# The next pair's first two mask products moved to one place, one of them in a score bank

## The chip, the cores and the metric

The kernel runs on one core of a Trainium2 chip. The metric is the time of one execution on the device, in microseconds (us). Four runs of the kernel before took 996.92 to 997.95 us, with a median of 997.31 us.

## What is computed

The reference has two stages. The first is routed attention over 4 batches, 8 heads, 768 positions and 64 dimensions. Each query and each key is assigned to the nearest of 16 centroids of its head, and a query sees only the keys of its own cluster. The second stage is a wide layer with the gate h * erf(softplus(h)).

```python
q_assign = np.argmax(np.einsum('bhsd,hcd->bhsc', q_n, c_n), axis=-1)
k_assign = np.argmax(np.einsum('bhsd,hcd->bhsc', k_n, c_n), axis=-1)
mask = q_assign[:, :, :, None] == k_assign[:, :, None, :]
scores = np.where(mask, scale * np.matmul(q, k.transpose(0, 1, 3, 2)), -1000000000.0)
attn = np.exp(scores - np.max(scores, axis=-1, keepdims=True))
attn = attn / (np.sum(attn, axis=-1, keepdims=True) + 1e-09)
x = np.matmul(attn, v)                      # then (3072, 512)
h = x @ w_in                                # (3072, 2048)
out = (h * erf(np.maximum(h, 0) + np.log1p(np.exp(-np.abs(h))))) @ w_out
```

## The kernel before

**Pairs, units, periods.** Two heads are worked on at a time, one on rows 0 to 63 and one on rows 64 to 127: 16 pairs, numbered p = 0 to 15. A pair has 12 units, one for each half of the 768 queries (384) and each block of 128 keys. `period` (line 756) does two units, u and u + 1, so a pair has six periods, i = 0 to 5; the text calls them the first to the sixth. The attention takes the first 400 us or so of the span; the wide layer follows and is not touched by the change.

**The order of the work is written out by hand.** Every instruction of the attention goes through `InOrder` (line 54, its call on line 62), which keeps program order on each engine. So almost every row of the profile says L62, and rows are told apart by their tiles. There is no scheduler that moves them.

**The mask as a product.** Cluster membership enters the scores as a second, small matrix product that is added to the first. For a query, `qm` holds its one-hot cluster code. For a key, `km` holds a very large negative number at all clusters but its own. `masks` (line 357) makes a half (384 columns) of `qm` or `km` of the next pair. A product of the constant `pick` with `hotT`, the one-hot codes turned on their side, puts the codes into a bank of the accumulation memory (PSUM), and the function returned then copies them from there into `qm` or `km`, in bf16. For queries the product reads rows 0 to 63 of the array, for keys rows 64 to 127. With `narrow` it reads only 32 of these rows, which lie beside those that other small products use.

**Banks.** PSUM has eight banks here: `turned[0]` and `turned[1]`, one each; `ps_s`, two buffers `sc` of two banks each for the score units; and `wide`, two banks. `turned[0]` and `turned[1]` in turn hold the attention sums of the two halves, the transposed maxima and the mask products.

**One period**, in program order:

- `turn` in the first and fourth periods: the row maxima found for the next half are transposed on TensorE and copied into one row of `qm` for each head, on ScalarE ("CAST qm<-turned 1x384").
- `step_ahead(u)`: for a block of queries of the half to come, bf16 products `wide<-kv,qv` and `wide<-km,qm`, and then a maximum over them on VectorE ("TENSOR_REDUCE nmx<-wide").
- `products` (line 431) of u and of u + 1: the fp32 products of queries and keys ("sc<-qT,kT"), for each head on its own 64 rows. An fp32 product runs in two passes and loads its own weights.
- `step_ahead(u + 1)` in three pieces, with the mask part `scores` (line 444) of u and of u + 1 between them ("sc<-qm,km").
- `curve` (line 458): the exponential on ScalarE ("ACTIVATE pr<-sc"), one for each unit.
- `accumulate` on GpSimd and `attend` on TensorE ("turned<-pr,in_v") for the two units of the period before.

The four mask products of the next pair are put in by the table `MASKS` (line 50): the first key half in the first period (place 3, between the scores of u and u + 1, in `turned[0]`, narrow, and copied by VectorE), the first query half in the third (place 0, ahead of the products, in `turned[1]`, copied by ScalarE), the second key half in the third and the second query half in the sixth (place 2, narrow, copied by ScalarE). The first pair has its own table, `FIRST_MASKS`.

**Weight steps.** Beside the attention, 22 pieces of the wide layer's weights are fetched and brought into another number form, two pieces in a pair, up to pair 11: `size` and `rest` on ScalarE, `bounded` and `shifted` on VectorE, `sign` on ScalarE, `summed` on GpSimd, which then has the next piece fetched. For piece n1 = 2p - 1, `size` and `rest` stand at the end of the second period, `bounded`, `sign` and `shifted` in the fourth and `summed` in the fifth.

Of the kernel before, what the change touches and what calls it, by code (L numbers as in the profile page):

```python
# [9 lines left out]
F32 = mybir.dt.float32  # L10
# [4 lines left out]
ALU = mybir.AluOpType  # L15
# [4 lines left out]
P = 128  # L20
# [10 lines left out]
NPAIR = B * HP  # L31
# [12 lines left out]
BIG = 2.0**60  # L44
# [2 lines left out]
NPT = NJ + 2  # L47
N_LATE = 10
LAST_X = 11
MASKS = {(0, 3): ("k", 0), (2, 0): ("q", 0), (2, 2): ("k", 1), (5, 2): ("q", 1)}  # L50
FIRST_MASKS = {(2, 0): ("k", 0), (2, 1): ("q", 0), (2, 2): ("k", 1), (5, 2): ("q", 1)}


# [17 lines left out]
def kernel(  # L71
# [13 lines left out]
    te, ve, ae, ge = (  # L85
        InOrder(tc, e, in_order) for e in (nc.tensor, nc.vector, nc.scalar, nc.gpsimd)
    )
# [8 lines left out]
    turned = [ps.tile([P, 512], F32, name=f"turned{i}") for i in range(2)]  # L96
# [12 lines left out]
    def passing(name, bufs, **kw):  # L109
        return attention.enter_context(tc.tile_pool(name=name, bufs=bufs, **kw))  # L110

    ps_s = passing("ps_s", 2, space=PSUM)
# [12 lines left out]
    nbig = const.tile([P, 1], F32, name="nbig")  # L125
# [71 lines left out]
    for base, pattern, sign, op, fill in (  # L197
# [5 lines left out]
            out=first, in_=first, compare_op=op, fill=fill, base=base, pattern=pattern,  # L203
# [31 lines left out]
    def size(n):  # L235
        ae.activation(out=w_steps[n][0], in_=steps[n][0], func=ACT.Abs, scale=UP)

    def rest(n):
        lo = steps[n][1]
        ae.activation(out=lo.bitcast(I32), in_=lo.bitcast(U32), func=ACT.Copy, scale=2.0**-29)  # L240

    def size_and_rest(n):
        size(n)
        rest(n)
# [109 lines left out]
        if p < NPAIR:  # L354
            ae.copy(out=pairs[p][nm + "v"], in_=pairs[p][nm + "T"])

    def masks(p, nm, half, bank, narrow=False, copied_by=ae):

        if p >= NPAIR:
            return lambda: None  # L360
        st = pairs[p]
        cols = slice(half * HW, (half + 1) * HW)
        r = slice(0, D) if nm == "q" else slice(D, P)
        if narrow:
            r = slice(r.start + half * Q, r.start + (half + 1) * Q)
        won = bank[:, 0:HW]
        te.matmul(won, lhsT=pick[r, half], rhs=st["hotT"][r], start=True, stop=True)
        if nm == "q":
            return lambda: ae.activation(out=st["qm"][:, cols], in_=won, func=ACT.Relu)
        if copied_by is ve:  # L370
            return lambda: ve.tensor_scalar(
                out=st["km"][:, cols], in0=won, scalar1=BIG, scalar2=nbig, op0=ALU.mult, op1=ALU.add
            )
        return lambda: ae.activation(
            out=st["km"][:, cols], in_=won, func=ACT.Identity, bias=nbig, scale=BIG
        )
# [3 lines left out]
    def maxima_step(p, i, sm=wide, behind=False):  # L380

        st = pairs[p]
        nmx = maxima[p % 2]
        t, half = divmod(i, 2)

        def passes(a, b, start, rows):
            for e in range(2):
                r = slice(e * D + rows.start, e * D + rows.stop)
                te.matmul(
                    sm[:, e, 0:HW], lhsT=st[a][r, t * P : (t + 1) * P],  # L390
                    rhs=st[b][r, half * HW : (half + 1) * HW], start=start, stop=not start,
                )

        passes("qv", "kv", True, slice(0, D))
        if behind:
            yield
        passes("qm", "km", False, slice(Q, D) if behind else slice(0, D))
        if behind:
            yield
        ve.tensor_reduce(  # L400
            out=nmx[:, :, t, half], in_=sm[:, :, 0:HW], axis=AX.X, op=ALU.max, negate=True
        )
        if i in (NJ - 1, 2 * NJ - 1):
            h = i // NJ
            ve.tensor_reduce(
                out=lowest[h][:, :, ::D].rearrange("p t e -> p e t"),
                in_=nmx[:, :, h * HJ : (h + 1) * HJ], axis=AX.X, op=ALU.min,
            )
            turns.append((p, h))
# [17 lines left out]
    units = [(p, half, j) for p in range(NPAIR) for half in range(2) for j in range(NJ)]  # L427

    sc_of = {}

    def products(u):
        p, half, j = units[u]
        if u in sc_of:
            return
        st = pairs[p]
        sc = sc_of[u] = ps_s.tile([P, 2, 512], F32, name="sc", tag="s")
        for e in range(2):
            r = slice(e * D, (e + 1) * D)
            te.matmul(
                sc[:, e, 0:HW], lhsT=st["kT"][r, j * P : (j + 1) * P],  # L440
                rhs=st["qT"][r, half * HW : (half + 1) * HW], start=True, stop=False,
            )
# [300 lines left out]
    def step_ahead(u, behind=False):  # L743
        p, i = divmod(u + NJ, 2 * NJ)
        steps = maxima_step(p, i, behind=behind) if p < NPAIR else iter(())
        if not behind:
            run(steps)
        return steps
# [7 lines left out]
    def period(p, i):  # L756
        u = 2 * NJ * p + 2 * i
        n1, n2 = 2 * p - 1, 2 * p
        early = lambda n: 0 <= n < N_EARLY

        def mask(place):
            which = (MASKS if p else FIRST_MASKS).get((i, place))
            if which:
                return masks(p + 1, *which, turned[0 if i in (0, 5) else 1], place > 1, ve if place == 3 else ae)
            return lambda: None

        if u > 0:
            for which in turns if i in (0, 3) else ():
                turn(*which)
                turns.remove(which)  # L770
            step_ahead(u)
        mask(0)()
        next(part[0], None)
        if i == 0 and p:
            run(routing[0])
        if u == 2:
            next(routing[0])
        products(u)
        products(u + 1)
        mask(1)()  # L780
        second = step_ahead(u + 1, True) if u > 0 else iter(())
        next(second, None)
        scores(u)
        next(second, None)
        mask(3)()
        next(second, None)
        next(part[0], None)
        scores(u + 1)
        later = mask(2)
        if i == 3:  # L790
            similarities(p + 2)
            routing[0] = choose(p + 2, sc_of[u + 1][:, 0])
        curve(u)
        later()
        curve(u + 1)
        if u == 0:
            step_ahead(1)
            similarities(1)
            routing[0] = choose(1, turned[0])
            next(routing[0])  # L800
            next(routing[0])
            vectors(1, "q")
            vectors(1, "k")
        if i == 0 and early(n1 - 1):
            bounded(n1 - 1)
            shifted(n1 - 1)
            sign(n1 - 1)
        elif i == 1 and early(n1):
            size_and_rest(n1)
        elif i == 3 and early(n1):  # L810
            bounded(n1)
            sign(n1)
        elif i == 5 and early(n2):
            rest(n2)
        for _ in range(min(len(forms), FORMS.get(p, {}).get(i, 0))):
            forms.pop(0)[0]()
        if i == 3:
            next(routing[0], None)
            if early(n1):
                shifted(n1)  # L820
            for _ in range(2):
                next(routing[0], None)
        elif i == 1:
            load(p + 1, "v", v, vp)
            if p == 0:
                run(routing[0])
                transposes(2, "q")
        elif i == 2:
            transposes(p + 2, "k")
        elif i == 4:  # L830
            vectors(p + 2, "k")
            vectors(p + 2, "q")
        elif i == 5:
            transposes(p + 3, "q")
        if u > 0:
            if i == 1 and early(n1 - 1):
                summed(n1 - 1)
            elif i == 4 and early(n1):
                summed(n1)
            for w in (u - 2, u - 1):  # L840
                accumulate(w)
            if i % HJ == 1 and p in POOL_FORMS and forms:
                forms.pop(0)[1]()
            for w in (u - 2, u - 1):
                attend(w)
            if i % HJ == 0:
                part[0] = divide(u - 1)
                next(part[0])
        if i == 3 and early(n2):
            size(n2)  # L850
# [11 lines left out]
    st = pairs[0]  # L862
    st["qT"], st["kT"] = rows[0]["q"], rows[0]["k"]
    ve.transpose(out=st["qT"], in_=st.pop("q").rearrange("p n t -> p (n t)"))
    for e in range(2):
        ve.tensor_copy(
            out=ccT[e * D : (e + 1) * D, :, e * C : (e + 1) * C],
# [8 lines left out]
    for r in (0, D):  # L876
        for half in range(2):
            for e in range(2):
                c = r + half * Q + e * C
                ve.tensor_copy(  # L880
                    out=pick[r : r + D, half, e * D : (e + 1) * D].rearrange("p (n c) -> p n c", n=2)[:, :, 1 : C + 1],
# [5 lines left out]
    run(choose(0))  # L887
    copies = [
        masks(0, nm, half, bank)
        for nm, half, bank in (("q", 0, wide[:, 0]), ("k", 0, turned[0]), ("k", 1, turned[1]))  # L890
    ]
# [30 lines left out]
    u = len(units)  # L922
# [107 lines left out]
```

## Time and profile before

| | us |
|---|---|
| median of four runs | 997.31 |
| the profiled execution | 997.32 |
| its span in the trace | 995.6 |
| TensorE matmuls busy (PE) | 987.6 (99%) |
| TensorE weight loads busy (PEld) | 743.0 (75%) |
| VectorE busy (DVE) | 700.8 (70%) |
| ScalarE busy (ACT) | 488.1 (49%) |
| GpSimd busy (POOL) | 350.3 (35%) |

The profile is that of one execution. Times are counted from the start of its span. A row of the timeline gives the start, the time from there to the end of the last instruction merged into it, the engine, the line, the operation, the tile written and the tiles read, shapes and count; in brackets stands how long the engine had been idle, and what ended that. A matmul's time reaches to the end of its way through the array, so back-to-back matmuls overlap in it, and products on different rows of the array run beside each other. Pairs 1 to 11 show the same rows, shifted by 24.59 us from pair to pair; the rows quoted later are mostly those of pairs 3 and 4.

### The profile page before, as it was taken

To read this page: it belongs to the slowest core of one execution; us is meant where nothing else is said; L and a number is where in the kernel's file an instruction comes from. 1 tells how busy PE (TensorE), PEld (TensorE's weight loads), DVE (VectorE), ACT (ScalarE), POOL (GpSimd) and SP (SyncE) were. 2 spreads that over 40 slices of the span, in tenths; PEclk is the share of its full clock that TensorE was granted. 3 is DMA by queue.
4 is the path that set the end of the run, shared out by engine and by line. 5 is a ranking of instruction groups with operands and counts; after the bars stand their busy time and mean duration, and the time that the engine had idled before them with its cause. 6 is when DMAs were issued, how large, how long until landed. Compare 5 with 4: busy or idle time off the path is not lost.

```text
span 995.6 us, 20543 instructions
## 1 busy us (share of the span) xinstructions
PE 987.6 (99%) x8362; PEld 743.0 (75%) x8362; DVE 700.8 (70%) x1347; ACT 488.1 (49%) x659; POOL 350.3 (35%) x237
## 2 busy tenths in 40 slices
PE   8999999999999999999999999999999999999998
PEld 3555555555555555688888888888888888888887
DVE  8888888888888776779676554756475647655653
ACT  3777777777776665475532324150505050505050
POOL 1677878778878888662400000000000000000000
PEclk9999999999999999999999999999999999999999
DMA  9444444444444210232000100010001000000001
GB/s 222 78 111 108 108 108 110 112 112 104 96 96 110 51 36 18 99 109 65 1 12 32 42 1 22 22 43 1 22 22 43 1 21 22 1 1 22 22 1 42
DMA packets 147294, 55.88 MB, mean 56 GB/s; under 512 B 128640, under 2 KB 137088, under 8 KB 147200
## 3 DMA queue, kind: packets, MB, share of 16 engines
q1 hardware_dynamic: 144848, 54.29, 21.8%
q8 instruction: 65, 1.06, 0.5%
q10 hardware_dynamic: 2352, 0.30, 0.2%
q14 instruction: 29, 0.24, 0.1%
HBM read 41.98 MB, written 12.58 MB: 55 GB/s over the span
## 4 chain that ended last, share of the span: by engine, by line
PE 96%; DVE 1%; POOL 1%; DMA 1%; issue 0%; ACT 0%; SPq 0%; ACTq 0%; DVEq 0%; POOLq 0%
PE bank L62 43%; PE turned L62 31%; PE sc L62 16%; PE wide L62 6%; POOL more_out L62 1%; DVE nmx L62 1%; DMA g_more<-in_moe_w_out_dram 0%; DMA in_q<-in_q_dram 0%; DVE sims L62 0%; POOL x_more L62 0%; DVE kT L62 0%; DVE qT L62 0%; ACT pr L62 0%; ACT w_out L62 0%; DVE turned L62 0%
## 5 line engine op out<-in xcount | busy, mean ns | idle before, releaser
L62 POOL TENSOR_TENSOR more_out<-more_out,pr 128x768 f32<-128x768 f32 x128 | 217.0, 1695 | 19.2 <-ACT pr L62 10.5
L62 DVE TENSOR_REDUCE nmx<-wide 128x2 f32<-128x768 f32 x189 | 180.7, 956 | 58.7 <-PE wide L62 57.6
L62 ACT ACTIVATE pr<-sc 128x768 f32<-128x768 f32 x192 | 148.9, 812 | 95.7 <-PE wide L62 91.0
L62 PE MATMUL turned<-pr,in_v 128*32 128x194 f32 x3072 | 145.5, 330 | 0.0
L62 PEld LDWEIGHTS turned<-pr,in_v 128*32 128x32 f32 x3072 | 91.5, 109 | 51.2 <-issue 21.3
L62 DVE TENSOR_TENSOR g<-bank,g 128x256 f32<-128x256 f32 x222 | 89.7, 422 | 53.2 <-PE bank L62 46.4
L62 PE MATMUL bank<-x_own,w_in 128*128 128x256 f32 x424 | 104.7, 380 | 1.1 <-DVE g L62 1.1
L62 PE MATMUL bank<-w_out,g 128*128 128x256 f32 x448 | 103.1, 379 | 0.0
L62 PE MATMUL sc<-qT,kT 64*128 64x384 f32 x528 | 98.3, 484 | 0.0
L62 PEld LDWEIGHTS bank<-w_out,g 128*128 128x128 f32 x448 | 85.1, 190 | 11.6
L62 PEld LDWEIGHTS bank<-x_own,w_in 128*128 128x128 f32 x424 | 80.3, 190 | 12.9 <-DVE g L62 1.5
L62 DVE TENSOR_TENSOR osb<-bank,osb 128x256 f32<-128x256 f32 x87 | 35.5, 421 | 72.8 <-ACT osb L62 25.4
L62 ACT COPY g<-bank 128x256 f32<-128x256 f32 x28 | 10.4, 372 | 153.0 <-PE bank L62 148.5
L62 ACT ACT_TABLE_LOAD x48 | 61.6, 1283 | 45.7 <-DVE g L62 45.1
L62 PE MATMUL bank<-x_more,more_in 128*128 128x256 f32 x296 | 76.0, 379 | 0.0
L62 POOL TENSOR_TENSOR more_out<-pr,pr 128x768 f32<-128x768 f32 x32 | 60.0, 1875 | 28.4 <-ACT pr L62 28.4
L62 PEld LDWEIGHTS sc<-qT,kT 64*128 64x128 f32 x528 | 51.8, 187 | 19.8 <-ACT inv L62 2.3
L62 PE MATMUL wide<-kv,qv 64*128 64x384 bf16 x378 | 64.9, 328 | 1.1 <-ACT km L62 0.6
L62 PEld LDWEIGHTS <-qv 64*128 64x128 bf16 x384 | 26.9, 93 | 51.8 <-issue 35.7
L62 PE MATMUL bank<-more_out,g_more 128*128 128x256 f32 x272 | 64.3, 379 | 0.0
L62 DVE TENSOR_TENSOR g<-a_s,g 128x512 f32<-128x512 f32 x96 | 62.5, 689 | 1.4 <-ACT a_s L62 1.4
L62 PE MATMUL wide<-km,qm 64*128 64x384 bf16 (+1 forms) x378 | 62.5, 327 | 0.0
(170 smaller groups left out, 1668.3 us busy)
## 6 DMA issues: line engine op xcount, KB each, us to landing
x_own<-in_moe_w_in_dram SPq DMA_DIRECT2D x13, 512.0 KB, 4.2
in_v<-in_v_dram SPq DMA_DIRECT2D x32, 192.0 KB, 3.0
x_dram<-more_out SPq DMA_DIRECT2D x128, 48.0 KB, 1.7
x_own<-x_dram SPq DMA_DIRECT2D x6, 1024.0 KB, 5.3
out_dram<-osb SPq DMA_DIRECT2D x23, 256.0 KB, 2.0
in_k<-in_k_dram SPq DMA_DIRECT2D x59, 96.0 KB, 2.7
in_q<-in_q_dram SPq DMA_DIRECT2D x58, 96.0 KB, 2.8
g_more<-in_moe_w_out_dram SPq DMA_DIRECT2D x6, 512.0 KB, 3.4
```

The lines of the kernel that those rows point to most:

```text
L62: ins = getattr(self.engine, name)(*args, **kw)
```

## The change

The first key mask leaves the first period and is put beside the first query mask, in the third period, ahead of the products. The query mask's product no longer goes to `turned[1]` but to the first bank of the score buffer of u, which is allocated early for it; the key mask's goes to `turned[1]`, on all 64 of its rows. Both are copied by ScalarE, the query's first. As u's fp32 product overwrites the bank of the query mask, the period's two products are made in turned order, that of u + 1 first. This holds for pairs 1 to 14; the first pair's table is unchanged, and the last pair makes no masks.

Two weight steps on ScalarE move with it, in the pairs that have them: `size` from the end of the second period to behind the two copies in the third, and `rest` to the fourth, ahead of its products. The copy by VectorE goes away, and so does the piece of `step_ahead` that made room for it: the order of the remaining instructions is the same there.

```diff
-MASKS = {(0, 3): ("k", 0), (2, 0): ("q", 0), (2, 2): ("k", 1), (5, 2): ("q", 1)}
+MASKS = {(2, 2): ("k", 1), (5, 2): ("q", 1)}
...
-        if copied_by is ve:
-            return lambda: ve.tensor_scalar(
-                out=st["km"][:, cols], in0=won, scalar1=BIG, scalar2=nbig, op0=ALU.mult, op1=ALU.add
-            )
...
         passes("qm", "km", False, slice(Q, D) if behind else slice(0, D))
-        if behind:
-            yield
...
+    multiplied = set()
+
+    def bank_of(u):
+        if u not in sc_of:
+            sc_of[u] = ps_s.tile([P, 2, 512], F32, name="sc", tag="s")
+        return sc_of[u]
...
     def products(u):
         p, half, j = units[u]
-        if u in sc_of:
+        if u in multiplied:
             return
+        multiplied.add(u)
         st = pairs[p]
-        sc = sc_of[u] = ps_s.tile([P, 2, 512], F32, name="sc", tag="s")
+        sc = bank_of(u)
...
-        products(u)
-        products(u + 1)
+        both = i == 2 and 0 < p < NPAIR - 1
+        if both:
+            copies = [masks(p + 1, "q", 0, bank_of(u)[:, 0]), masks(p + 1, "k", 0, turned[1])]
+            for copy in copies:
+                copy()
+            if early(n1):
+                size(n1)
+        if i == 3 and early(n1):
+            rest(n1)
+        for w in (u + 1, u) if both else (u, u + 1):
+            products(w)
         mask(1)()
         second = step_ahead(u + 1, True) if u > 0 else iter(())
         next(second, None)
         scores(u)
-        next(second, None)
-        mask(3)()
         next(second, None)
...
-        elif i == 1 and early(n1):
-            size_and_rest(n1)
```

More of the change, by code (lines that the diff above doesn't have):

```diff
@@ L355, in vectors, with masks @@
             ae.copy(out=pairs[p][nm + "v"], in_=pairs[p][nm + "T"])
-    def masks(p, nm, half, bank, narrow=False, copied_by=ae):
+    def masks(p, nm, half, bank, narrow=False):
         if p >= NPAIR:
@@ L763, in mask @@
             if which:
-                return masks(p + 1, *which, turned[0 if i in (0, 5) else 1], place > 1, ve if place == 3 else ae)
+                return masks(p + 1, *which, turned[0 if i in (0, 5) else 1], place > 1)
             return lambda: None
```

## The prediction

> **What bounds the kernel now.** I read the page's chain of work that ended last first, then the busy table of chosen stretches, then the timeline of single periods.
>
> ```profile
> span 995.6 us, 20543 instructions
> PE 96%; DVE 1%; POOL 1%; DMA 1%; issue 0%; ACT 0%; SPq 0%; ACTq 0%; DVEq 0%; POOLq 0%
> ```
>
> TensorE is 96% of the chain that ended last, and its granted clock is at the top digit in all 40 slices. So a change counts by what it adds to or takes from TensorE's own stream. Copies on ScalarE and VectorE count only where TensorE waits for them.
>
> The edit acts in 14 pairs (p = 1 to 14), in the first and the third of their six periods. What the two mask products cost there is seen by setting pair 4 beside pair 15, which has no next pair and so no masks. The stretches run from one period's first score product (qm with km) to the next period's; columns: stretch, its length, then busy time of each engine.
>
> ```profile
> 118.81:123.06 4.25, 4.25 (x63) 2.44 (x61) 3.69 (x8) 3.28 (x5) 1.91 (x2) 1.00 0.61 114
> 388.49:392.58 4.09, 4.09 (x63) 2.34 (x63) 2.90 (x5) 2.30 (x4) 2.92 (x3) 1.00 0.00 0
> 123.06:126.99 3.93, 3.93 (x55) 2.50 (x54) 2.96 (x5) 3.01 (x5) 3.80 (x3) 1.00 0.87 225
> 392.58:396.34 3.76, 3.76 (x54) 2.08 (x53) 2.92 (x5) 1.51 (x2) 3.31 (x3) 1.00 0.11 27
> ```
>
> The first two rows hold the key mask of the first period: 4.25 against 4.09, so it costs 0.16 us. The last two hold the query mask of the third period: 3.93 against 3.76, about 0.16 us too. TensorE is busy throughout all four, though pair 15 gives VectorE 0.8 us less to do in the first of them: nothing else waits there.
>
> **Removed: the key mask's place in the first period.** It goes from between the scores to beside the query mask: 14 x 0.16 = 2.24 us off the path. Its copy on VectorE (14 x 0.62 us) was off the path: the maxima that stood behind it ended at 120.91, and TensorE came to the next product into that bank at 121.19. Taking it away is worth nothing.
>
> **Added beside the query mask: the key mask, on the other 64 rows.** The set-up at the start shows such a pair.
>
> ```profile
> 11.29 0.32 PE L62 MATMUL wide<-hotT,pick 64*128 64x384 bf16 x1
> 11.30 0.50 PE L62 MATMUL turned<-hotT,pick 64*128 64x384 bf16 x2
> ```
>
> Three mask products: the query one on rows 0 to 63 and a key one on rows 64 to 127 start within 0.01 us, and only the third comes 0.17 later. So the second mask is taken at nothing beyond the 0.16 that the query mask pays today. In today's third period the upper rows just run 0.16 us ahead for that time and wait at the period's end.
>
> **Added: a wait.** The query mask now lies in the first half of unit u's score bank, so u's product may overwrite it only after ScalarE has copied it. The turned order puts u+1's product in front as cover. How long is the copy, and how long the cover? In pairs 12 to 14 ScalarE has no weight steps, and the same copy starts as soon as the mask is there, as it will after the change:
>
> ```profile
> 322.00 0.32 PE L62 MATMUL turned<-hotT,pick 64*128 64x384 bf16 x1
> 322.36 0.49 ACT L62 ACTIVATE qm<-turned 128x384 bf16<-128x384 f32 x1 [0.62 <-PE turned L62]
> ```
>
> With M for the mask's start, the copy runs from M + 0.36 to M + 0.85. TensorE then has to be released. The nearest row is a weight load that waits for a reduction, 0.05 us after its end (103.82 + 0.19 = 104.01, load at 104.06):
>
> ```profile
> 103.82 0.19 DVE L62 TENSOR_REDUCE lowest<-nmx 128x6 bf16<-128x18 f32 x1
> ...
> 104.06 0.29 PEld L62 LDWEIGHTS <-lowest 128*32 128x32 bf16 x6
> ...
> 104.79 1.45 PE L62 MATMUL sc<-qT,kT 64*128 64x384 f32 x8
> ```
>
> So the load for u's product starts at M + 0.90. The last row above sizes the cover: two units are eight fp32 passes in four side-by-side pairs; with 0.48 us for one pass (the page's mean is 484 ns) the pairs stand (1.45 - 0.48) / 3 = 0.323 us apart, and one unit holds TensorE for 0.645. Without a wait, u's product would begin at M + 0.16 + 0.645 = M + 0.81. It cannot: the copy alone is late.
>
> Two smaller terms come on top. The wait stands at the load itself (fp32 products load their own weights), so the load is bare. The only row of a bare fp32 load is in the set-up:
>
> ```profile
> 18.95 0.30 PEld L62 LDWEIGHTS sc<-qT,kT 64*128 64x128 f32 x4
> 18.96 0.92 PE L62 MATMUL sc<-qT,kT 64*128 64x384 f32 x4
> ```
>
> One unit took 0.92 us there, against 0.323 + 0.48 = 0.81 in the stream: 0.11 us more. And after a wait the second half's load starts 0.03 us behind the first's (two loads took 0.12 us at 12.32, after a wait for a mask copy, against 0.09 to 0.10 elsewhere). u's product therefore starts at M + 0.90 + 0.11 + 0.03 = M + 1.04, a **stall of 0.23 us**, of which nothing is given back: the score products, the sums over keys and the next period follow directly.
>
> A rule bears on the 0.11. The Trainium skill, "TensorE: Matmul & The Clock Gate", section "Part 2: What happens when you issue a matmul", says that TensorE's queue pulls weight loads ahead of matmuls in flight. By that the load would be done during the cover, the stall would be 0.12 us and the sum 14 x (0.12 - 0.16) = -0.6 us. The row speaks against it: in the fifth period the second fp32 unit waits, and the trace shows no load of it until 110.05, when the wait ends.
>
> **Moved: two weight steps on ScalarE** (11 of the pairs). `size` (0.67 us) goes from the second period's end to the third, behind the two mask copies and ahead of u's exponential. Query copy to 101.55, key copy (0.57) to 102.1, `size` to 102.7; the exponential started at 102.84 and, with the stall, is due at 103.07. The cover is 0.3 us; were it gone, each 0.1 us late would pass on whole, since the fourth period's first product waits for the key copy between the exponentials (ends 104.13, product at 104.18, just when TensorE comes to it). `rest` (0.69 us) goes to the fourth period, behind the two one-row copies that end at 105.65: done by 106.34, and the exponential is due at 106.80. Their users are VectorE at 107.66 and GpSimd at 109.65. DMA issues on SP and GpSimd's steps keep their order, and the buffers come free at the same step. Cost: nothing.
>
> **The sum.** Per pair -0.16 + 0.23 = +0.07; 14 x 0.07 = +1.0 us. The profiled execution took 997.32 us (span 995.6), which is the median of the four runs shown (997.31). Forecast **998.3 us**, 0.1% more: the change swaps one TensorE slot for a wait a little longer.
>
> Bounds of the stall. Below: the load is not bare and the second half not late, 0.90 - 0.81 = 0.09, sum -1.0 us, 996.3. Above: the release takes 0.12 (the hot comparison ended at 109.93, the fp32 load that waited for it and another stands at 110.05) instead of 0.05: stall 0.30, sum +2.0, 999.3. I take 0.23, because the copy is the same instruction in the same state and the release a single one.
>
> **Rivals.** (A) *The wait is hidden.* Then 2.24 us are gained: 995.1 us. For it: u+1's product is 0.645 us long and the copy 0.49. Against: the mask's result takes 0.36 to reach the copy, so the copy would have to end at M + 0.65, and the row has M + 0.85. (B) *The stall is bigger, and the kernel slower.* Place: u's product in the third period. Price: if the two halves' bare loads (0.19 each) come one after the other and the release takes 0.12, the stall is 0.85 + 0.12 + 0.38 - 0.81 = 0.54, sum 14 x 0.38 = +5.3 us, 1002.6. It decides from a stall of 0.30 on. For it: no row shows a bare fp32 load in the middle of the stream. Against: in the set-up the two halves' loads ran together. (C) *The masks do not run side by side.* Then they hold TensorE 0.32 us, but the cover starts 0.16 later by M while the copy does not, so the stall shrinks to 0.07: again +0.07 per pair, 998.3. The copy's end sets the time either way, and only the rows would tell.
>
> **How the numbers follow.** About 0.2% (2 us) is what a measurement of this kernel can tell from no change. Forecast with the bounds of its stall 0.68, C 0.06 (both within 0.2%), A 0.10 (faster, just past the line), B 0.16 (slower). Range: 996.3 to 999.3 with the scatter of the runs before (996.92 to 997.95, some 0.5 to a side): 995.8 to 999.9. Parts of A and B are left out.
>
> **What would show it.** In the profile after: the first period's stretch at 4.09 in place of 4.25; the third's at about 4.16 (3.93 + 0.23); the query copy starting 0.36 after its mask in all pairs, and a TensorE weight load that waits for it; the two masks within 0.01 us; u's exponential released by TensorE, not by ScalarE's own queue. I am wrong if TensorE shows no wait there (A), if the waiting product's two halves start 0.19 apart (B), or if an exponential starts late behind `size` or `rest`.

## The result, and the profile after

The changed kernel took **998.38 us** (median of 41 runs, 997.92 to 998.83), the kernel before 997.23 us (median of 61 runs, 996.77 to 998.52): a ratio of 1.001, with a 95% interval of 1.0006 to 1.0015. That is 1.15 us more, within 0.2%. The profiled execution of the changed kernel took 998.57 us; that of the kernel before took 997.32.

From the page after, the span and the shares of the chain that ended last:

```profile
span 996.9 us, 20504 instructions
...
PE 96%; DVE 1%; POOL 1%; DMA 1%; ACT 0%; issue 0%; ACTq 0%; DVEq 0%; POOLq 0%
```

TensorE is still 96% of the chain. The span is 1.3 us longer, with 39 instructions fewer. So the answer has to be found inside TensorE's stream, stretch by stretch. The busy table of chosen stretches after, pair 4 (columns: stretch; length; busy time of PE, PEld, DVE, ACT and POOL, each followed by its count of instructions; granted clock; DMA share; GB/s). The last row is the stretch of the third row, one pair earlier:

```profile
119.29:123.38 4.09, 4.09 (x63) 2.35 (x62) 3.08 (x7) 3.26 (x5) 1.75 (x2) 1.00 0.62 116
123.38:127.50 4.12, 4.12 (x56) 2.00 (x54) 3.10 (x6) 3.04 (x5) 3.96 (x4) 1.00 0.83 221
127.50:131.71 4.21, 4.12 (x61) 2.36 (x60) 3.08 (x4) 3.44 (x6) 4.05 (x3) 1.00 0.25 52
...
102.87:106.81 3.94, 3.94 (x63) 2.36 (x62) 3.07 (x4) 3.45 (x6) 3.78 (x3) 1.00 0.21 42
```

First row: 4.09 in place of 4.25, as wide as in pair 15, which has no mask there. Second row: 4.12 in place of 3.93. PE is called busy throughout, though TensorE waits inside it: a matmul's time reaches to the end of its way through the array, and that covers a wait of 0.2 us. A stretch's length tells more than its busy time here. Third row: the stretch from the third to the fourth period, which the prediction left unchanged, is 4.21 in pair 4 and 3.94 in pair 3, and only there does PE fall short of the length.

From the starts of single rows, in us (before, then after):

| stretch | pairs 1 to 14 | the exceptions |
|---|---|---|
| first to second period | 4.251, 4.090 (-0.162) | none |
| second to third period | 3.924, 4.128 (+0.204) | none |
| third to fourth period | 3.932, 3.932 (0) | pair 1: 4.253 (+0.32); pair 4: 4.206 (+0.275) |
| all others of these pairs | the same within 0.003 | none |

The sum is 14 x (0.204 - 0.162) = +0.59, and 0.32 + 0.275 = +0.60 from the two exceptions: **+1.19 us, of 1.15 measured**.

The timeline of the third period of pair 12 after shows the wait itself:

```profile
322.93 0.32 PE L62 MATMUL sc<-hotT,pick 64*128 64x384 bf16 x1
...
322.94 0.32 PE L62 MATMUL turned<-hotT,pick 64*128 64x384 bf16 x1
323.10 1.66 PE L62 MATMUL sc<-qT,kT 64*128 64x384 f32 x8
...
323.29 0.49 ACT L62 ACTIVATE qm<-sc 128x384 bf16<-128x384 f32 x1 [0.62 <-PE turned L62]
...
323.83 0.30 PEld L62 LDWEIGHTS sc<-qT,kT 64*128 64x128 f32 x4 [0.55 <-ACT qm L62]
```

The two mask products start together here (within 0.004 us in pairs 12 to 14, 0.003 to 0.022 us apart over all pairs). The copy starts 0.36 after its mask and lasts 0.49. The eight fp32 passes take 1.66 us, against 1.45 in the stream. The last row is the release: the weight load of the waiting unit starts 0.05 after the copy's end (323.29 + 0.49 = 323.78), and its bracket names the copy. The waits of TensorE's load queue, summed over the kernel, have a group for it that was not there before (us in all, times, the longest in us):

```profile
PEld sc L62 <- ACT qm L62: 7.5, 14, 0.5
```

Fourteen waits, one for each of pairs 1 to 14. Their 0.5 us each is idle time of the load queue, not the stall: for most of it the passes of u + 1 run.

What is new and was not foreseen is in the chain of work of pair 4, where ScalarE stands in a chain that is else TensorE's:

```profile
128.06 0.16 issue
128.22 0.81 ACT pr L62
129.03 0.48 ACT km L62
129.51 0.04 issue
129.55 0.34 PE turned L62 x6
```

"issue" is time in which the engine waited for nothing that the profile shows. The exponential of u (pr) starts late, the key copy behind it (km) ends late, and the fourth period's first product waits for that. ScalarE's timeline, pair 3 and pair 4, has the same exponential:

```profile
103.31 0.82 ACT L62 ACTIVATE pr<-sc 128x768 f32<-128x768 f32 x1 [0.47 <-PE wide L62]
...
128.22 0.81 ACT L62 ACTIVATE pr<-sc 128x768 f32<-128x768 f32 x1 [0.74 <-PE turned L62]
```

From the period's first score product it starts 0.436 later in pair 3 and 0.712 later in pair 4 (0.756 in pair 1). The wait instruction ahead of it is through after 0.39 in all fourteen pairs (its record starts 0.374 to 0.375 after the score product), and in pair 4 ScalarE had been idle for 0.74 us.

### The profile page after: what moved, and what is told of

It reads as the page before. It is cut to its first block, busy times and chain, and to the rows that moved or that the text cites. A ratio compares the mean times of both kernels' runs of the same rounds, so it can differ in the third digit from the quotient of the medians.

```text
span 996.9 us, 20504 instructions
## 1 busy us (share of the span) xinstructions
PE 988.6 (99%) x8362; PEld 734.7 (74%) x8362; DVE 694.2 (70%) x1333; ACT 497.3 (50%) x673; POOL 348.6 (35%) x237
## 4 chain that ended last, share of the span: by engine, by line
PE 96%; DVE 1%; POOL 1%; DMA 1%; ACT 0%; issue 0%; ACTq 0%; DVEq 0%; POOLq 0%
PE bank L62 43%; PE turned L62 31%; PE sc L62 16%; PE wide L62 6%; POOL more_out L62 1%; DVE nmx L62 1%; DMA g_more<-in_moe_w_out_dram 0%; ACT pr L62 0%; DMA in_q<-in_q_dram 0%; DVE sims L62 0%; POOL x_more L62 0%; DVE kT L62 0%; DVE qT L62 0%; ACT km L62 0%; ACT w_out L62 0%
## 5 line engine op out<-in xcount | busy, mean ns | idle before, releaser
L62 PEld LDWEIGHTS sc<-qT,kT 64*128 64x128 f32 x528 | 47.5, 186 | 25.4 <-ACT qm L62 4.8
L62 PE MATMUL wide<-kv,qv 64*128 64x384 bf16 x378 | 62.8, 328 | 1.1 <-ACT km L62 0.6
```

The lines of the kernel that those rows point to most:

```text
L62: ins = getattr(self.engine, name)(*args, **kw)
```

## The experiments

Each was run beside the kernel before, on the same chip; "before" is the median of those runs.

**The question** of the first ones: what makes one instruction late in two pairs of fourteen that run the same rows? *Theory:* ScalarE's instructions come in blocks, and an instruction whose place in the program is the first of a block starts some 0.3 us late. *Rivals:* the data or a queue make it late (the weight pieces of these two pairs, their DMAs), or the new wait does. Counting all of ScalarE's instructions in the trace, waits and DMA issues included, from 1, the late exponential is number 64 in pair 1 and 192 in pair 4, 128 apart. In the kernel before it is number 65 and 193, and the place 64 or 192 holds the separate semaphore wait ahead of it, where ScalarE idles anyway.

### e1_code_place: one more ScalarE instruction ahead of it

```diff
+    spare_one = const.tile([P, 1], F32, name="spare_one")
...
             vectors(1, "k")
+            ae.copy(out=spare_one, in_=alleps)
```

> The changed kernel with one more ScalarE instruction, a copy of one column, in the first pair. In the changed kernel the exponential of u in the third period starts late in pairs 1 and 4 only (by 0.32 and 0.28 us, and the fourth period comes that much later). These two are 128 instructions apart in ScalarE's program. Theory: a block of ScalarE's code ends just ahead of them, and the next instruction is had late. One instruction more moves the block's end to a place where ScalarE has time: both late starts go, the stretch from the third to the fourth period is 3.93 us in every pair, and the time is 0.6 us less, 997.8. Rival: the late starts come from the moved steps, a DMA or a wait on another engine in those pairs; then they stay, and the time is 998.4.

998.96 us, before 997.04; ratio 1.002 (1.0011 to 1.0029). The time missed, the rows did not: the third-to-fourth stretch is 3.932 in all pairs, pairs 1 and 4 too, and the second-to-third is 4.129. But the set-up ahead of the first pair is 1.22 us longer (first score product at 21.03, 19.81 after the change), and this covers the miss: 0.59 + 1.22 = 1.81, of 1.92 measured. The DMAs of `in_k` landed 4.7 us after issue there, and 3.4 in the changed kernel (medians over the first 9 us), and VectorE's transposes waited for them. The edit had a side effect: it adds a tile of 4 bytes a row ahead of other buffers. So it was made again without a tile.

### e1b_code_place: the same without a new tile

```diff
             vectors(1, "k")
+            ae.copy(out=minus[:, 0:1], in_=minus[:, 1:2])
```

> The changed kernel with one more ScalarE instruction in the first pair, this time a copy of one column of a constant onto another of the same value, so that no new buffer moves the others. In the first try the late starts of pairs 1 and 4 were gone, but the set-up took 1.2 us longer, as its first loads landed later. Theory: without the new buffer the set-up is as in the changed kernel (first score product at 19.8), the late starts stay away, and the time is 998.4 - 0.6 = 997.8. Rival (the instruction itself costs the set-up time): 999.0 again.

997.68 us, before 997.02; ratio 1.0007 (0.9998 to 1.0016). The set-up is back at 19.81, and the three stretches are 4.089, 4.129 and 3.932 in all fourteen pairs. Both late starts are gone, by an instruction that stands 30 us ahead of the first of them (at 23.39) and has no part in it. The sum without them is +0.59; measured are +0.66, and as the interval takes in 1, it is the rows that show it. No data, DMA or wait of pairs 1 and 4 was changed: these rivals fall.

### e2_before_code_place: the late starts put into the kernel before

```diff
-            vectors(1, "k")
+            ge.tensor_copy(out=pairs[1]["kv"], in_=pairs[1]["kT"])
```

> The kernel before with one ScalarE instruction fewer ahead of pair 1: a copy for the second pair's keys is made on GpSimd in the first pair, where GpSimd has nothing else to do. That puts the exponential of u of the third period of pairs 1 and 4 just behind the end of a block of code, as the change did. Theory of the code's place: both start some 0.3 us late although nothing else of the change is there; 997.25 + 0.6 = 997.85. Rival (moved steps, a DMA, a wait): no late start, 997.25.

One copy in the first pair goes from ScalarE to GpSimd, so that all later instructions of ScalarE move up one place. 997.72 us, before 997.04; ratio 1.0007 (0.9998 to 1.0016). The interval takes in 1, so the clock alone does not show it; the rows do. Second-to-third and third-to-fourth stretch of pair 4 in the busy table, and ScalarE's timeline in pair 1:

```profile
123.39:127.31 3.92, 3.92 (x55) 2.50 (x55) 2.95 (x5) 3.01 (x5) 3.80 (x3) 1.00 0.85 229
127.31:131.52 4.21, 4.12 (x61) 2.35 (x62) 3.08 (x4) 2.78 (x5) 4.02 (x3) 1.00 0.26 53
```

```profile
53.98 0.81 ACT L62 ACTIVATE pr<-sc 128x768 f32<-128x768 f32 x1 [1.21 <-PE turned L62]
```

The first is 3.92, as in the kernel before: no new wait. The second is 4.21 (4.238 in pair 1), and 3.932 in all other pairs. The exponential starts after ScalarE has idled for 1.21 us. So the late starts need nothing of the change but its count of instructions.

Over all kernels, with the exponential's number in pair 1 and pair 4 and the third-to-fourth stretch:

| kernel | numbers | pair 1 | pair 4 |
|---|---|---|---|
| before, e5 | 65, 193 | 3.93 | 3.93 |
| after | 64, 192 | 4.253 | 4.206 |
| e1, e1b, e6, e7, e10 | 65, 193 | 3.93 | 3.93 |
| e2 | 64, 192 | 4.238 | 4.207 |
| e3 | 64, 192 | 4.234 | 4.207 |
| e8 | 64, 195 | 4.249 | 3.932 |
| e9 | 64, 192 | 4.234 | 4.207 |

e8 tells most: there only pair 1 falls on the place, and only pair 1 is late. In the changed kernel the next such numbers, 320 and 448, fall on the exponential of u + 1 in pair 7, which is started while ScalarE is still busy, and on a one-row copy in pair 10; neither period is longer.

The same place further on gives the same late start to other exponentials. In e8, number 448 is the exponential of u in the second period of pair 10; in e1b, number 576 is that of the fifth period of pair 13, and so it is in e1, e6 and e10:

```profile
273.50 0.81 ACT L62 ACTIVATE pr<-sc 128x768 f32<-128x768 f32 x1 [1.20 <-PE sc L62]
```

```profile
358.22 1.51 ACT L62 ACTIVATE pr<-sc 128x768 f32<-128x768 f32 x2 [1.65 <-PE sc L62]
```

They start 0.713 and 0.715 after the period's first score product, in all other pairs 0.435 to 0.437. No period is longer for it, so nothing that bounds TensorE waits for these two. e1b has thus not done away with late starts: one stands where it costs nothing.

### e3_natural_order: the change without the turned order

```diff
-        for w in (u + 1, u) if both else (u, u + 1):
+        for w in (u, u + 1):
```

> The changed kernel with the third period's products in natural order, u ahead of u + 1, so that nothing covers the copy of the query mask. Theory of the exposed copy: u's product still starts 1.01 us after the mask, but would be due 0.16 us after it; the stall is 0.85 us, the stretch from the second to the third period 4.13 + 0.645 = 4.77, and the time 998.4 + 14 x 0.645 = 1007.4. Rival (the turned order makes the stall): the time falls below 998.4.

1007.16 us, before 997.02; ratio 1.0104 (1.0088 to 1.0119). The second-to-third stretch is 4.774, 0.645 more than after, and 0.645 is what the prediction gave for the cover that u + 1's product makes. TensorE's waits:

```profile
PEld sc L62 <- ACT qm L62: 13.5, 14, 1.0
...
PE sc L62 <- ACT qm L62: 7.9, 14, 0.6
```

The second line is absent after the change: without cover the matmuls themselves stand idle, 0.6 us in each pair. (In the profiled execution of e3 the set-up is 0.34 us shorter than after the change, with the first score product at 19.47; the cause is open.)

### e5_turned_order_alone: the kernel before with the turned order

```diff
-        products(u)
-        products(u + 1)
+        for w in (u + 1, u) if i == 2 and 0 < p < NPAIR - 1 else (u, u + 1):
+            products(w)
```

> The kernel before with the turned order alone: in the third period of pairs 1 to 14, u + 1's product ahead of u's, and the masks where they were. Theory: the order by itself costs nothing, since the buffer of u + 1 is free (its exponential ended 0.2 us before the load that needs it); 997.2, all stretches as before (3.92 from the second to the third period). Rival (the turned order takes part in the stall): a longer stretch there, and up to 997.2 + 14 x 0.2 = 1000.

997.03 us, before 997.06; ratio 1.0 (0.9991 to 1.0009), all stretches as before. The order by itself costs nothing.

### e7_weight_steps_stay: the two weight steps left in the second period

```diff
-            if early(n1):
-                size(n1)
-        if i == 3 and early(n1):
-            rest(n1)
...
+        elif i == 1 and early(n1):
+            size_and_rest(n1)
```

> The changed kernel with the two weight steps on ScalarE left at the end of the second period, as in the kernel before. Theory of the exposed copy: in pairs 1 to 11 the query copy then stands behind them and starts 0.74 us after its mask, as it did in the kernel before, and not 0.36; the stall grows by 0.38 in these 11 pairs (stretch from the second to the third period 4.51) and not in pairs 12 to 14 (4.13): 998.4 + 11 x 0.38 = 1002.6. Rival (the steps' place does not matter): 998.4.

1001.83 us, before 997.06; ratio 1.0049 (1.0033 to 1.0066). Timeline, pair 4:

```profile
126.41 0.32 PE L62 MATMUL sc<-hotT,pick 64*128 64x384 bf16 x1
...
126.59 0.67 ACT L62 ACTIVATE x_own<-x_own 128x512 int32<-128x512 uint32 x1
...
127.16 0.47 ACT L62 ACTIVATE qm<-sc 128x384 bf16<-128x384 f32 x1
...
127.68 0.30 PEld L62 LDWEIGHTS sc<-qT,kT 64*128 64x128 f32 x4 [0.90 <-ACT qm L62]
```

The weight step holds ScalarE when the mask is there, the copy starts 0.75 after its mask instead of 0.36, and the load waits 0.90. The second-to-third stretch is 4.50 to 4.53 in pairs 1 to 11, which have such steps, and 4.129 in pairs 12 to 14, which have none: all of the 0.38 lands on TensorE. 14 x 0.042 + 11 x 0.38 = +4.8, as measured. The expectation was 0.8 too high, and for 0.6 of it the theory gives the reason: with the steps back in the second period the exponential is number 65 and 193 again, and the late starts are gone.

### e8_key_mask_stays: the key mask left in the first period

```diff
-MASKS = {(2, 2): ("k", 1), (5, 2): ("q", 1)}
+MASKS = {(0, 3): ("k", 0), (2, 2): ("k", 1), (5, 2): ("q", 1)}
...
-            copies = [masks(p + 1, "q", 0, bank_of(u)[:, 0]), masks(p + 1, "k", 0, turned[1])]
+            copies = [masks(p + 1, "q", 0, bank_of(u)[:, 0])]
```

(With it, VectorE's copy and the piece of `step_ahead` that the change took away are back.)

> One part of the change alone: the query mask in the score bank and the turned order, but the key mask left in the first period, on 32 rows and copied by VectorE as before. Theory of the exposed copy: the whole stall is there without the key mask's product (stretch from the second to the third period 4.13) and the first period's slot is not saved (4.25): 997.25 + 14 x 0.20 = 1000.1. Rival: the key mask's product beside the query mask makes part of the stall; then the stretch is shorter than 4.13 and the time less than 1000.

1000.15 us, before 997.04; ratio 1.0031 (1.0019 to 1.0043). First-to-second 4.251, second-to-third 4.130: the third period is as long with the query mask alone as with both (4.128). So the second mask beside the first costs nothing that these stretches show, and the 0.162 that goes from the first period is a true gain. 14 x 0.206 + 0.32 = +3.2, of 3.11 measured.

### e6_masks_earlier: both masks ahead of the second maxima product

```diff
-            step_ahead(u)
+            if i == 2 and 0 < p < NPAIR - 1:
+                ahead = step_ahead(u, True, False)
+                next(ahead)
+            else:
+                step_ahead(u)
...
+            run(ahead)
             for copy in copies:
                 copy()
```

(Here `run(ahead)`, which issues the rest of `step_ahead`, stands between the mask products and their copies; `step_ahead` is cut into two pieces, with all rows kept; the instruction and the tile of e1 are in it too.)

> The changed kernel with the one-column copy of the other run, and the two mask products put 0.16 us earlier: between the two products of the first maxima step of the third period. Theory of the exposed copy: the query mask starts 0.16 us earlier against the slot of u's product, so the stall falls from 0.20 to some 0.04 to 0.07 us, the stretch from the second to the third period goes from 4.13 to about 3.98, and the time is 998.4 - 0.6 - 14 x 0.15 = 995.7. Rival: the 0.20 us come from the turned order or from the two masks beside each other; then nothing is gained over the one-column copy alone, 997.8.

998.17 us, before 997.04; ratio 1.0012 (1.0003 to 1.0021). A partial miss. The second-to-third stretch is 3.966 in pairs 12 to 14, as good as the expected 3.98, but 4.09 to 4.11 in pairs 1 to 11, and the set-up is 1.36 us longer, as with the tile of e1. Timeline, pair 4 (the first three rows) and pair 12:

```profile
125.97 0.54 DVE L62 SCALAR_TENSOR_TENSOR more_out<-den,turned 128x384 f32<-128x384 f32 x1
...
126.38 0.32 PE L62 MATMUL sc<-hotT,pick 64*128 64x384 bf16 x1
...
126.57 0.32 PE L62 MATMUL turned<-hotT,pick 64*128 64x384 bf16 x1
...
323.22 0.32 PE L62 MATMUL sc<-hotT,pick 64*128 64x384 bf16 x1
...
323.22 0.32 PE L62 MATMUL turned<-hotT,pick 64*128 64x384 bf16 x1
```

In pair 4 the key mask waits for VectorE, which reads the attention sums from its bank `turned[1]` until 126.51, and starts 0.19 after the query mask; in pair 12 VectorE is earlier and both start together. The idea was right, but the key mask's bank is not free that early. So only the query mask should go earlier; it has a bank of its own.

### e9_query_mask_first: the query mask at the head of the period, the key mask where it is

```diff
+            if i == 2 and 0 < p < NPAIR - 1:
+                copies = [masks(p + 1, "q", 0, bank_of(u)[:, 0])]
             step_ahead(u)
...
-            copies = [masks(p + 1, "q", 0, bank_of(u)[:, 0]), masks(p + 1, "k", 0, turned[1])]
+            copies.append(masks(p + 1, "k", 0, turned[1]))
```

> The changed kernel with the query mask's product at the head of the third period, ahead of the first maxima step, and the key mask's product left behind that step. In the run with both masks earlier the key mask waited for VectorE's last use of its bank in pairs 1 to 11, and held the queue. The two products no longer start together, but each only delays its own 64 rows. Theory of the exposed copy: the query mask is 0.33 us earlier against u's product, the wait is gone, the stretch from the second to the third period is 3.76 + 0.16 = 3.93, and only the two late starts of the changed kernel remain: 997.25 - 14 x 0.16 + 0.6 = 995.6. Rival (two masks must start together to cost one slot): 4.09 and 997.9.

995.80 us in a single run, before 997.02. Second-to-third 3.930 to 3.948; the late starts are there (4.234 and 4.207).

### e10_query_mask_first_code_place: e9 with the instruction of e1b

> The same with the one-column copy that moves the end of ScalarE's block of code. Theory: no stall, no late start, 997.25 - 14 x 0.16 = 995.0, less than both kernels. Rival (two masks must start together to cost one slot): 997.3.

**995.05 us**, before 997.02; ratio 0.9981 (0.9972 to 0.999): 1.97 us less than before, so it beats both kernels. The busy table, first-to-second and second-to-third stretch of pair 12:

```profile
314.01:318.10 4.09, 4.09 (x62) 2.34 (x61) 3.00 (x6) 2.30 (x4) 3.01 (x3) 1.00 0.60 112
318.10:322.03 3.93, 3.93 (x56) 2.19 (x55) 2.93 (x5) 2.48 (x4) 3.48 (x3) 1.00 0.49 101
```

The first period's slot is saved, and the stretch to the third is 3.930, against 3.924 before the change. Timeline:

```profile
319.98 0.33 PE L62 MATMUL sc<-hotT,pick 64*128 64x384 bf16 x1
...
320.32 0.32 PE L62 MATMUL turned<-hotT,pick 64*128 64x384 bf16 x1
320.35 0.49 ACT L62 ACTIVATE qm<-sc 128x384 bf16<-128x384 f32 x1 [0.30 <-PE sc L62]
320.48 1.46 PE L62 MATMUL sc<-qT,kT 64*128 64x384 f32 x8
...
320.89 0.43 PEld L62 LDWEIGHTS sc<-qT,kT 64*128 64x128 f32 x4 [0.22 <-ACT qm L62]
```

The query mask has moved 0.34 ahead of the key mask, and its copy with it. The load still waits for the copy, but the eight passes take 1.46, as without a wait: the load is now done while u + 1's passes run. In pairs 1 to 11 the stretch is 0.02 longer than before; that was not followed up.

## Why the prediction was right, and where it was wrong

The forecast was 998.3 us; measured were 998.38. The time came out, but partly by luck, for in it two errors nearly cancel: the saved slot and the stall were to give +1.0 and gave +0.59, while a step that was priced at nothing gave +0.60. The mechanism of the stall was right; the other half of the time came from something that the prediction did not have.

- **The key mask's place in the first period, -0.16:** right, -0.162 in all 14 pairs. e8, with the mask left there, keeps 4.251.
- **The second mask at nothing beside the first:** right. They start 0.003 to 0.022 us apart, and e8 has the same third period with one mask. Rival C is out.
- **The copy from M + 0.36 to M + 0.85, the release 0.05 later, the cover to M + 0.81:** right within 0.01 (pair 12: copy from M + 0.359 to M + 0.849, load at M + 0.900, u + 1's product done with at M + 0.808). e3, which takes the cover away, lengthens the period by just its 0.645.
- **The bare fp32 load, 0.11:** right, 0.105 (a pass with it takes 0.587 us, 0.482 without).
- **The second half 0.03 late:** mis-sized. The two halves' loads start 0.007 apart (323.833 and 323.840). The 0.03 was read off two loads of another product, after another wait (in the fifth period of pair 3 before, two waiting fp32 loads do start 0.035 apart, at 110.046 and 110.081). The stall is 0.900 + 0.105 + 0.007 - 0.808 = 0.204, not 0.23, and the net per pair +0.042, not +0.07.
- **Moved weight steps "Cost: nothing":** this step failed. Their place in time was right: the third period's exponential of u starts as before, 0.436 after the first score product, but for two pairs, and e7, which leaves the steps where they were, costs 0.38 in each of 11 pairs. But moving instructions also changes their numbers. The exponential went from 65 to 64 in pair 1 and from 193 to 192 in pair 4, and starts 0.32 and 0.275 late there. As the prediction said, what is late there passes on whole: the fourth period comes 0.32 and 0.275 later. e1b takes it from these two by one instruction, and e2 brings it into the kernel before. The prediction looked for a late exponential "behind `size` or `rest`"; it was late behind an idle engine.
- **VectorE's copy worth nothing, the turned order worth nothing:** nothing speaks against the first (the first period's gain is that of the mask product alone), and e5 shows the second.
- **The rule of the Trainium skill** on loads pulled ahead ("TensorE: Matmul & The Clock Gate", "Part 2: What happens when you issue a matmul") did not take the load past the wait. Where nothing waits, the rows agree with it: in pair 12 the load of the second fp32 pass starts at 323.10, its pass at 323.42. But no load of u's product is seen before the copy's end. By the rule, as the prediction applied it, the stall would be about 0.10 (an estimate: 0.204 less the 0.105 of the bare load).
- **Rivals:** A (hidden) and B (0.54) are both out; the stall was within its bounds of 0.09 and 0.30. What A asked for, a copy that ends earlier, is had by issuing the mask earlier (e10).

That the late start is the fetch of the next block of instructions is **argued, not shown**. For it: the place, 64 and then 128 instructions further each time, in every kernel; and in the DMA records an instruction packet of 8,192 bytes, 64 for each of 128 instructions, is on its way soon after each late start (at 54.97 and 128.87 in the changed kernel, 0.93 and 0.65 us after; at 274.16 in e8 and 358.88 in e1b, 0.66 us after). Such packets come 74 us apart and are put down to ScalarE, whose 128 instructions are three pairs. In e1b, where number 64 and 192 are the separate waits ahead of the exponential, the packets stand at 51.39 and 124.60, 1.9 and 2.6 us ahead of the period's first score product. The Trainium skill, "Runtime: NRT & Kernel Launch", section "Instruction fetch mechanics", says that an engine's instruction memory is refilled in blocks of 16 KiB, 256 instructions, and that crossing a boundary costs one DMA tail bump, "mostly hidden". The runs agree in that there are places with a price; they lie 128 apart on ScalarE here, not 256, and where ScalarE is the next on the path the price is not hidden. The fetch itself has no row in the trace. That the tile makes the loads of the set-up land later rests on e1 and e6, which have it, against e1b, which differs from e1 in it; why was not tried.

## What to carry to other kernels

Price a wait by its whole chain (product to copy, copy, release, bare load) against the time of what is put in front of it, and, if it comes out short, start the chain earlier before adding cover: 0.34 us earlier was worth nearly all of the stall here (4.128 to 3.930 in pairs 12 to 14, 3.924 before). Leave a moved step at "nothing" only after asking what else it shifts; when a few periods of many equal ones are late behind an idle engine and an "issue" in the chain, count the instructions up to them and shift the count by one. An edit for an experiment should not allocate: a tile of 4 bytes a row cost twice as much as the effect that it was to show.

## What was not expected of the hardware

- ScalarE starts an instruction 0.27 to 0.32 us late at numbers 64, 192, 448 (e8) and 576 (e1b) of its trace, where the one ahead of it was a separate wait and the engine was idle.
- A new tile of 4 bytes a row ahead of the other buffers made the first loads of `in_k` land 4.7 us after issue in place of 3.4, and the set-up 1.2 to 1.4 us longer.
- A waiting fp32 product holds back its own weight load, and in the 14 waits of the changed kernel both halves' loads then start within 0.007 us of each other.
